# An adaLN transformer block on one core: the condition vector loaded as one row, its silu placed between the layernorm statistics, and one planned step moved later

## The chip, the core and the metric

The kernel runs on 1 core of one Trainium2 chip. The metric is the time of one execution on the device in microseconds (us). Before the change it is 761.05 us, the median of 3 runs (759.68 to 762.66). About half a per cent, 3.8 us, can be told from no change with such runs.

Names used throughout: PE is the matrix engine (PEld its weight load), DVE the vector engine, ACT the scalar engine, POOL the general engine, SP the engine that here only issues transfers. Each of them works through a list of instructions of its own, in order. SPq, ACTq and POOLq in a view are the issues of transfers by SP, ACT and POOL.

## What is computed

A block of 2048 tokens of width 512: layernorm, modulated by a condition vector c; attention with 32 heads of 16; a gated residual; again a modulated layernorm; a feed-forward layer of 1376 with gelu; a gated residual.

```python
mod = (_silu(c) @ w_mod).reshape(c.shape[0], 6, 1, -1)
sa, ca, ga, sb, cb, gb = (mod[:, i].copy() for i in range(6))
h = _layernorm(x, axis=-1) * (1 + ca) + sa
x = x + ga * _A_ref(h, A_wqkv, A_wo)      # softmax attention, then wo
h = _layernorm(x, axis=-1) * (1 + cb) + sb
x = x + gb * _B_ref(h, B_w1, B_b1, B_w2, B_b2)   # gelu MLP
return x
```

c has 512 numbers. Only sa and ca (the first 1024 columns of w_mod) are needed before the first attention scores; the rest of mod is needed later.

## The kernel before

**Tiling.** Tokens are in four blocks b of 512 (four tiles of 128), the width in four chunks of 128 (NC = 4). Activations are kept transposed (hT, kT: width on the partitions, tokens along the row). A *quad* is four heads of equal parity in one chunk for one token block; there are 32 quads of 16 key tiles, the last four of them in halves.

**Prologue (lines 128 to 384), written in order by hand.** SP and ACT each issue two tiles of x block 0 (line 140) and half of W_m0, the first 1024 columns of w_mod (line 143). Between the two, POOL issues the load of c into cc_bf, four numbers on each of 128 partitions (line 141): element j*128 + p of c goes to partition p, column j. PE meanwhile runs WARM[0] = 16 products of zeros (turn_over, line 348); WARM[1] is not used. DVE makes small masks from pidx, which POOL writes after its issue of c, and then takes the statistics of the four x tiles (line 353). Behind the second of these, SP's next loads are released: W_k, W_q, x block 1, W_v, x blocks 2 and 3, and a further part of w_mod (lines 355 to 362). ln_rstd aggregates them on DVE (line 203) and takes the root on POOL (lines 208 and 209). Then silu_c (lines 181 to 186): exp(-c) on ACT, and add, reciprocal and product on DVE give sc_bf. first_mod_mm (line 231) multiplies the columns of W_m0 with sc_bf in 32 one-column products on PE, into psm, a part of PSUM bank 7. Then for each x tile DVE normalises (line 217) and PE transposes (line 371); first_mod (lines 246 and 247) and hT_evac (lines 257 and 260) apply the modulation; PE makes the first k and q (line 379). So on PE's list stand, in order: the warming products, the 32 products with W_m0, sixteen transposes, eight products with W_k and W_q.

**The planned part (from line 386).** All that follows is ordered by a planner which runs when the program is built. It keeps a clock for each engine (`clk`), gives every step a duration in ns, and at each moment emits a step for the engine whose clock stands earliest. A dictionary `rdy` says from which time on a result may be used; a step is emitted only when all that it needs is ready by these times. So a number in `rdy` sets where in an engine's list the step that uses the result will stand, and on the chip the step waits there for the true event. Score tiles are computed by PE (line 902) and turned into weights by ACT with exp (line 1379, two or three tiles at once) or by DVE with integer arithmetic (lines 1523 and 1557). Which of the two gets a tile is decided as the plan goes, from DVE's planned load. PE then multiplies with the values (line 1141) into bank 7. Zero products (line 1222) are put in where PE would be idle.

**End of a quad (emit_out, line 1462).** DVE copies the result to o_sb (line 1472). The row of sums goes to DRAM (line 1477, d1) and back as a 128-partition piece `dall` (line 1479), both issued by SP. `rdy[("dall", qi)]` (line 1487) says when DVE may take the reciprocal (line 1491, in `back`); its result goes to DRAM and is spread over the partitions in `rb` (lines 1493 and 1496). When that is due (6500 ns later by the plan), POOL multiplies (line 1500) and adds (line 1503) into OT, which the output projection of the block uses later.

**open_late (line 556)** is a planned POOL step, run once when the weights of the prologue are no longer needed. It issues the loads of W_1 and W_2 (1376 and 1280 KB) on ACT's list and four small loads on SP's (lines 567 to 575).

Of the kernel before, what the change touches and what calls it, by code (L numbers as in the profile page):

```python
# [12 lines left out]
BF16 = mybir.dt.bfloat16  # L13
FP32 = mybir.dt.float32
# [6 lines left out]
P = 128  # L21
S = 2048
D = 512
F = 1376
H = 32
NC = 4
# [38 lines left out]
ROOT = 1000.0  # L65
ROOT_L = 700.0
SPREAD = (0.9, 0.9, 0.65)
WARM = (16, 3)
FRONT = (1200.0, 0.0, 2600.0, 4000.0)
AHEAD = 32  # L70
T_KEEP = 3
# [22 lines left out]
def adaln_block(ctx: ExitStack, tc: tile.TileContext, A_x, A_wqkv, A_wo, B_x, B_w1, B_b1, B_w2, B_b2,  # L94
                c, w_mod, out):
    nc = tc.nc
# [3 lines left out]
    const = ctx.enter_context(tc.tile_pool(name="const", bufs=1))  # L100
# [4 lines left out]
    kT = res.tile([P, NC, S], BF16, name="kT")  # L105
# [17 lines left out]
    def load_mod(i, eng):  # L123
        t = prom.tile([P, NC, 2 * D], BF16, name="W_m")
        eng.dma_start(out=t, in_=wm_v[:, :, 2 * i * D:2 * (i + 1) * D])
        return t

    xb = [prox.tile([P, 4, D], BF16, name="xb") for _ in range(NQB)]
    cc_bf = const.tile([P, NC], BF16, name="cc_bf")
# [5 lines left out]
    still = kT[:, NC - 1, S - 512:S]  # L135
    nc.vector.memset(still, 0.0)
    W_m0 = prom.tile([P, NC, 2 * D], BF16, name="W_m")
    for i, eng in enumerate((nc.sync, nc.scalar)):
        for t in (2 * i, 2 * i + 1):
            eng.dma_start(out=xb[0][:, t, :], in_=x_tok[0][:, t, :])  # L140
    nc.gpsimd.dma_start(out=cc_bf, in_=c.rearrange("o (j p) -> p (o j)", p=P))
    for i, eng in enumerate((nc.sync, nc.scalar)):
        eng.dma_start(out=W_m0[:, 2 * i:2 * i + 2, :], in_=wm_v[:, 2 * i:2 * i + 2, 0:2 * D])

# [33 lines left out]
    scf = const.tile([P, NC], FP32, name="scf")  # L178
    scb = prow.tile([P, NC, P], BF16, name="scb")

    def silu_c():
        ce = const.tile([P, NC], FP32, name="ce")
        nc.scalar.activation(out=ce, in_=cc_bf, func=ACT.Exp, scale=-1.0)
        nc.vector.tensor_scalar(out=ce, in0=ce, scalar1=1.0, scalar2=None, op0=ALU.add)
        nc.vector.reciprocal(out=ce, in_=ce)
        nc.vector.tensor_tensor(out=sc_bf, in0=cc_bf, in1=ce, op=ALU.mult)
# [25 lines left out]
    def ln_rstd(st, n):  # L212
        mv = ln_mean(st, n)
        return mv, ln_root(mv, n)
# [26 lines left out]
    def first_mod_mm(ps):  # L241
        mod_cols(ps, W_m0, 0, 0)
        mod_cols(ps, W_m0, D, 4)
# [85 lines left out]
    def bk(i, dt=FP32, n=512):  # L329
        if dt is BF16:  # L330
            return PS[:, i, 0:n // 2].bitcast(BF16)
        return PS[:, i, 0:n]
# [12 lines left out]
    dall = const.tile([P, NQB * 8, 16], FP32, name="dall")  # L345
    def turn_over(n):
        for _ in range(n):
            nc.tensor.matmul(out=PS[0:32, 6, :], lhsT=zero, rhs=still, start=True, stop=True)

    turn_over(WARM[0])  # L350
    st0 = pron.tile([P, 12, 6], FP32, name="st1")
    for t in range(4):
        seen = nc.vector.bn_stats(out=st0[:, t, :], in_=xb[0][:, t, :])
        if t == 1:
            held = nc.sync.dma_start(out=W_k, in_=wqkv_v[:, :, D:2 * D])
            tc.add_manual_dep(held.ins, seen.ins.name, AFTER, reason="order of loads")
            nc.sync.dma_start(out=W_q, in_=wqkv_v[:, :, 0:D])
            nc.sync.dma_start(out=xb[1], in_=x_tok[1])
            nc.sync.dma_start(out=W_v, in_=wqkv_v[:, :, 2 * D:3 * D])
            for b in range(2, NQB):  # L360
                nc.sync.dma_start(out=xb[b], in_=x_tok[b])
            W_m1 = load_mod(1, nc.sync)
    psm = bk(7, FP32, 16)
    mv0, rs0 = ln_rstd(st0, 4)
    silu_c()
    first_mod_mm(psm)
    turned = [bk(2 + j, BF16) for j in range(NC)]
    for t in range(4):
# [43 lines left out]
    rdy = {}  # L412
# [14 lines left out]
    def op(eng, dur, fn, label, needs=(), pos=0):  # L427
        s = Step("op", eng, dur, fn, needs, label, pos)
        alone.append(s)
        return s  # L430
# [122 lines left out]
    for j in range(NC):  # L553
        op("POOL", 1220.0, gate(lambda: W_o, j, ga_b), ("wo", j), ["ga"] + ([("wo", j - 1)] if j else []))

    def open_late():
        pro.close()
        lw = ctx.enter_context(tc.tile_pool(name="latew", bufs=1, side="right"))
        W_1 = lw.tile([P, NC, FPAD], BF16, name="W_1")
        nc.gpsimd.memset(W_1[:, :, F:FPAD], 0.0)  # L560
        nc.scalar.dma_start(out=W_1[:, :, 0:F], in_=B_w1.rearrange("(j p) n -> p j n", p=P))
        W_2 = lw.tile([P, NFC, D], BF16, name="W_2")
        lr = F - (NFC - 1) * P
        nc.gpsimd.memset(W_2[:, NFC - 1, :], 0.0)
        nc.scalar.dma_start(out=W_2[:, 0:NFC - 1, :],
                            in_=B_w2[0:(NFC - 1) * P, :].rearrange("(j p) n -> p j n", p=P))
        nc.sync.dma_start(out=W_2[0:lr, NFC - 1, :], in_=B_w2[(NFC - 1) * P:F, :])
        b1_bf = lw.tile([P, NFC], BF16, name="b1_bf")
        nc.gpsimd.memset(b1_bf, BIG)
        nc.sync.dma_start(out=b1_bf[:, 0:NFC - 1], in_=B_b1[0:(NFC - 1) * P].rearrange("(j p) -> p j", p=P))  # L570
        nc.sync.dma_start(out=b1_bf[0:lr, NFC - 1:NFC],
                          in_=B_b1[(NFC - 1) * P:F].rearrange("(p o) -> p o", o=1))
        b1c = lw.tile([P, NFC], FP32, name="b1c")
        nc.gpsimd.tensor_copy(out=b1c, in_=b1_bf)
        nc.sync.dma_start(out=W_2[lr:lr + 1, NFC - 1, :], in_=B_b2.rearrange("(o f) -> o f", o=1))
        nc.gpsimd.tensor_scalar(out=W_2[lr:lr + 1, NFC - 1, :], in0=W_2[lr:lr + 1, NFC - 1, :], scalar1=1.0 / BIG,
                                scalar2=None, op0=ALU.mult)
        clk["ACT"] += 120.0
        late.update(W_1=W_1, W_2=W_2, b1c=b1c)
        tl = ctx.enter_context(tc.tile_pool(name="tailp", bufs=1, side="right"))  # L580
        tl2 = ctx.enter_context(tc.tile_pool(name="tailp2", bufs=2, side="right"))
        late.update(tl=tl, tl2=tl2)
# [270 lines left out]
    clk = {"PE": 0.0, "ACT": 650.0, "DVE": 950.0, "POOL": 0.0}  # L853
# [608 lines left out]
    def emit_out(qi, t):  # L1462
        hf = None if qi < LAST else (qi - LAST) // HV
        if hf is not None and (qi - LAST) % HV >= HV - 2:
            return emit_half(qi, t)
        b, tq = quads[qi]
        ch, par = divmod(tq, 2)
        cs = tok_of(qi)
        n = cs.stop - cs.start
        f = n // 32  # L1470
        o = osp.tile([P, 512], FP32, name="o_sb")
        made = nc.vector.tensor_copy(out=o[:, cs], in_=PS[:, 7, cs])  # L1472
        clk["DVE"] = t + 67.0 + 1.042 * n
        dve_log.append((clk["DVE"], made))
        od_free[0] = clk["DVE"] + L_DVE
        d1 = scr.tile([4, n], FP32, name="d1" if hf is None else "dh")
        nc.sync.dma_start(out=d1, in_=o.rearrange("(r e) n -> r e n", e=32)[:, 16 - par, cs])
        den = dall[:, tq + 8 * b, f * (hf or 0):f * (hf or 0) + f]
        nc.sync.dma_start(out=den, in_=d1.rearrange("r (p f) -> (r p) f", f=f))
        rb = RB[par]  # L1480
        if par == 0 and not hf:
            if (b, ch) == (1, 0) and FIRST < NC:
                OT[(b, ch)] = odp.tile([P, 512], BF16, name="OT1")
            else:
                OT[(b, ch)] = otp.tile([P, 512], BF16, name="OT")
        ot = OT[(b, ch)]
        rdy[("dall", qi)] = clk["DVE"] + 6000.0

        def back():
            rp = osp.tile([P, 16], FP32, name="rp")  # L1490
            nc.vector.reciprocal(out=rp[:, 0:f], in_=den)
            d2 = scr.tile([4, n], FP32, name="d2" if hf is None else "di")
            nc.sync.dma_start(out=d2.rearrange("r (p f) -> (r p) f", f=f), in_=rp[:, 0:f])
            for r in range(4):
                rows = slice(32 * r + 16 * par, 32 * r + 16 * par + 16)
                nc.sync.dma_start(out=rb[rows, cs], in_=d2[r:r + 1, :].to_broadcast([16, n]))
            rdy[("rb", qi)] = clk["DVE"] + 6500.0

        def mult():
            return nc.gpsimd.tensor_tensor(out=(o if par else ot)[:, cs], in0=o[:, cs], in1=rb[:, cs], op=ALU.mult)  # L1500

        def both():
            return nc.gpsimd.tensor_tensor(out=ot[:, cs], in0=ot[:, cs], in1=o[:, cs], op=ALU.add)  # L1503

        long = 60.0 + 2.27 * n
        alone.insert(0, Step("op", "DVE", 170.0, back, [("dall", qi)], ("rp", qi)))
        alone.insert(0, Step("op", "POOL", long, mult, [("rb", qi)], ("oo" if par else "oe", b, ch, hf)))
        if par:
            alone.insert(0, Step("op", "POOL", long, both, [("oe", b, ch, hf), ("oo", b, ch, hf)],
                                 ("ot", b, ch) if hf is None else ("ot", b, ch, hf)))  # L1510
# [180 lines left out]
    while cur[0] < QN or outs or sums or evacs or alone:  # L1691
        e = min(clk, key=lambda x: (clk[x], rank[x]))
        t = clk[e]
# [51 lines left out]
```

## Time and profile before

| | us |
|---|---|
| median of 3 runs | 761.05 |
| the profiled execution | 759.09 |
| its span, first to last instruction | 757.2 |
| PE busy | 737.4 |
| ACT busy | 720.6 |
| DVE busy | 701.0 |
| POOL busy | 110.6 |

The profile is of one execution. Times in it are from the span's start. A row of the timeline is: start, duration, engine, line of the kernel, operation, output<-input, shape, count; in brackets the time for which the engine was idle before it, and what ended that. A row of the windows is: stretch, its length, busy time of PE, PEld, DVE, ACT and POOL with counts, the granted PE clock (1.00 is full), the busy share of the 16 DMA engines, and GB/s. The chain of waits is followed back from the last instruction, at each step to whatever released it.

### The profile page before, as it was taken

What the parts mean: (1) busy time and instruction counts of PE and PEld (TensorE: products, weight loads), DVE (VectorE), ACT (ScalarE), POOL (GpSimd) and SP (SyncE); (2) the same over time, 40 slices, a digit from 0 to 9 for tenths busy, and PEclk for the clock granted to TensorE, in tenths of its full rate; (3) what the DMA queues carried; (4) which work ended last, traced back from release to release, by engine and by line L of the source; (5) the groups of instructions that cost most, each with busy time, mean ns of one, the idle gap of its engine ahead of it and who ended that gap; (6) DMA issues with size and microseconds to landing.
All of it is one profiled execution on the core that took longest, in us unless ns stands there. A gap on an engine that the chain in (4) does not pass through costs nothing.

```text
span 757.2 us, 21449 instructions
## 1 busy us (share of the span) xinstructions
PE 737.4 (97%) x8885; PEld 259.4 (34%) x8888; DVE 701.0 (93%) x1455; ACT 720.6 (95%) x732; POOL 110.6 (15%) x137
## 2 busy tenths in 40 slices
PE   6999999999899999999999999999999999999997
PEld 3432333233233333223332232332233322444444
DVE  4966999999799999999999999999999999999984
ACT  1999999999899999999999999999999999999993
POOL 3334100211032311101001110100101110010010
PEclk8999999999999999999999999999999999999999
DMA  8300000000500100000001000000001000000000
GB/s 281 109 2 3 16 5 11 7 10 21 148 10 9 38 9 3 10 9 10 17 13 48 10 10 9 10 6 24 22 11 51 10 24 10 17 22 14 5 9 31
DMA packets 27960, 20.49 MB, mean 27 GB/s; under 512 B 14049, under 2 KB 23906, under 8 KB 27858
## 3 DMA queue, kind: packets, MB, share of 16 engines
q1 hardware_dynamic: 25442, 15.57, 7.2%
q10 hardware_dynamic: 2384, 3.51, 1.5%
q8 instruction: 71, 1.16, 0.6%
q14 instruction: 31, 0.25, 0.1%
q0 software_dynamic: 32, 0.00, 0.0%
HBM read 16.45 MB, written 2.61 MB: 25 GB/s over the span
## 4 chain that ended last, share of the span: by engine, by line
PE 64%; ACT 22%; DVE 5%; issue 5%; DMA 2%; SPq 0%; DVEq 0%; ACTq 0%
PE PS L902 22%; PE PS L1141 21%; ACT PB L1379 21%; PE PS L435 14%; PE PS L1222 3%; DVE TB L1523 3%; DVE TB L1557 2%; PE PS L770 2%; PE PS L799 1%; DMA W_m<-in_w_mod_dram 1%; DMA d<-o_sb 1%; ACT uG L649 1%; PE PS L1225 1%; PE PS L222 1%; ACT L1379 0%
## 5 line engine op out<-in xcount | busy, mean ns | idle before, releaser
L1379 ACT ACTIVATE PB<-PS 128x1024 bf16<-128x1024 f32 (+1 forms) x687 | 673.3, 1211 | 8.3 <-PE PS L902 4.6
L1523 DVE TENSOR_SCALAR TB<-PS 128x512 int16<-128x512 f32 (+1 forms) x538 | 369.5, 700 | 11.7 <-PE PS L902 9.5
L902 PE MATMUL PS<-qm,kT 32*128 32x512 bf16 (+1 forms) x2304 | 293.2, 359 | 5.4 <-ACT PB L1379 4.0
L1141 PE MATMUL PS<-PB,VE 128*32 128x512 bf16 (+1 forms) x1654 | 254.0, 361 | 0.0
L1141 PE MATMUL PS<-TB,VV 128*32 128x512 f16 (+1 forms) x1252 | 221.3, 360 | 1.8 <-DVE TB L1557 1.8
L1557 DVE TENSOR_SCALAR TB<-TB 128x1024 int16<-128x1024 int16 x556 | 219.9, 419 | 3.3
L902 PEld LDWEIGHTS <-kT 32*128 32x128 bf16 x2304 | 83.1, 91 | 253.6 <-issue 249.0
L1141 PE MATMUL PS<-TB,VE 128*32 128x512 f16 (+2 forms) x650 | 148.6, 361 | 0.2 <-DVE TB L1523 0.2
L1141 PEld LDWEIGHTS <-VE 128*32 128x32 bf16 x2304 | 72.4, 94 | 81.3 <-issue 75.3
L1222 PE MATMUL PS<-W_q,zero 128*32 128x256 bf16 x497 | 96.2, 274 | 1.3 <-DVE TB L1523 0.9
L1141 PEld LDWEIGHTS <-VV 128*32 128x32 bf16 x1252 | 57.3, 95 | 39.9 <-issue 36.6
L1222 PEld LDWEIGHTS <-zero 128*32 128x32 bf16 x497 | 46.0, 96 | 33.7 <-issue 11.1
L1500 POOL TENSOR_TENSOR OT<-o_sb,rb 128x512 bf16<-128x512 f32 (+1 forms) x16 | 19.3, 1203 | 248.4 <-DVE TB L1557 134.8
L1500 POOL TENSOR_TENSOR o_sb<-o_sb,rb 128x512 f32<-128x512 f32 (+1 forms) x16 | 19.3, 1204 | 223.4 <-DVE TB L1557 204.4
L435 PE MATMUL PS<-h2T,W 128*32 128x512 bf16 x528 | 47.3, 383 | 0.0
L435 PE MATMUL PS<-W,uG 128*32 128x512 bf16 x528 | 46.4, 383 | 0.0
L639 DVE TENSOR_SCALAR uG<-PS,b1c 128x512 bf16<-128x512 f32 x33 | 24.5, 742 | 0.0
L1503 POOL TENSOR_TENSOR OT<-OT,o_sb 128x512 bf16<-128x512 bf16 (+1 forms) x16 | 17.6, 1100 | 32.3 <-DVE TB L1557 30.1
L435 PE MATMUL PS<-W_o,OT 128*32 128x512 bf16 x272 | 22.2, 383 | 0.0
L1472 DVE COPY o_sb<-PS 128x512 f32<-128x512 f32 (+1 forms) x32 | 20.7, 647 | 0.9 <-PE PS L1141 0.8
L308 POOL TENSOR_SCALAR VV<-VE 128x512 bf16<-128x512 bf16 x12 | 18.0, 1502 | 20.7 <-DVE VE L303 12.5
L435 PE MATMUL PS<-hT,W_k 128*32 128x512 bf16 x240 | 20.9, 385 | 0.0
(124 smaller groups left out, 418.0 us busy)
## 6 DMA issues: line engine op xcount, KB each, us to landing
rb<-d SPq DMA_DIRECT2D x112, 32.0 KB
W_m<-in_w_mod_dram SPq DMA_DIRECT2D x2, 1024.0 KB
out_dram<-ob SPq DMA_DIRECT2D x16, 128.0 KB
xb<-in_A_x_dram SPq DMA_DIRECT2D x3, 512.0 KB
xr<-in_A_x_dram SPq DMA_DIRECT2D x3, 512.0 KB
W<-in_B_w_dram ACTq DMA_DIRECT2D x1, 1376.0 KB
W<-in_B_w_dram ACTq DMA_DIRECT2D x1, 1280.0 KB
W_m<-in_w_mod_dram ACTq DMA_DIRECT2D x1, 512.0 KB
```

What stands on the lines that cost most here:

```text
L308: return nc.gpsimd.tensor_scalar(out=dst, in0=src, scalar1=WJ[j], scalar2=None, op0=ALU.mult)
L435: nc.tensor.matmul(out=ps[cols, :], lhsT=lhsT[:, cols], rhs=rhs, start=start, stop=stop)
L639: return lambda ps, e: nc.vector.tensor_scalar(out=T["u"][:, fc, :], in0=ps, scalar1=late["b1c"][:, fc:fc + 1], scalar2=None, op0=ALU.add)
L902: nc.tensor.matmul(out=bk(bank)[:, seg(qi, i)], lhsT=kT[32 * r:32 * r + 32, ch, kt[i] * P:(kt[i] + 1) * P], rhs=qm[(b, ch)][32 * r:32 * r ...
L1141: nc.tensor.matmul(out=PS[32 * r:32 * r + 32, 7, tok_of(qi)], lhsT=wt, rhs=src[:, seg(qi, i)], start=not started[qi][r], stop=todo[qi][r] ...
L1222: nc.tensor.matmul(out=PS[0:32, b_, 0:256], lhsT=zero, rhs=W_q[:, 0, 0:256], start=True, stop=True)
L1379: nc.scalar.activation(out=dst, in_=PS[:, b0:b0 + n, :], func=ACT.Exp, bias=-KEXP * math.log(2.0), scale=math.log(2.0) / STEP)
L1472: made = nc.vector.tensor_copy(out=o[:, cs], in_=PS[:, 7, cs])
L1500: return nc.gpsimd.tensor_tensor(out=(o if par else ot)[:, cs], in0=o[:, cs], in1=rb[:, cs], op=ALU.mult)
L1503: return nc.gpsimd.tensor_tensor(out=ot[:, cs], in0=ot[:, cs], in1=o[:, cs], op=ALU.add)
L1523: made = nc.vector.tensor_scalar(out=TB[:, u["a"]["s"], i:i + n, :], in0=PS[:, b0:b0 + n, :], scalar1=T_BIAS, scalar2=0.0, op0=ALU.add, op ...
L1557: made = nc.vector.tensor_scalar(out=TB[:, s, 0:n, :], in0=TB[:, a["s"], 0:n, :], scalar1=float(MJ[j] - MJ[j - 1]), scalar2=None, op0=ALU.add)
```

## The change

Five edits, in three places.

- *The load of c.* It becomes one row of 512 numbers on one partition (cc_row, a piece of kT that is written later), issued first on ACT's list instead of on POOL's. A one-element tile `one` is set by DVE.
- *Row to columns.* Four products of a 1x128 piece of the row with `one` put c on 128 partitions, four columns, into columns 8 to 11 of psm (silu_in); DVE copies them to cc_bf (silu_exp).
- *Order of silu.* The copy and the exp come after the first of the four statistics, the rest (silu_out) after the third.
- *Warming products.* 6 before silu_in and 9 behind it, instead of 16.
- *A due time in the plan.* open_late notes POOL's planned time. A quad copied out between 4 us before and 14 us after it has its sums due 11 us after the copy instead of 6 us.

```diff
-WARM = (16, 3)
+WARM = (6, 9)
...
+    cc_row = kT[0:1, NC - 2, S - D:S]
+    one = const.tile([1, 1], BF16, name="one")
+    nc.vector.memset(one, 1.0)
+    nc.scalar.dma_start(out=cc_row, in_=c)
     for i, eng in enumerate((nc.sync, nc.scalar)):
         for t in (2 * i, 2 * i + 1):
             eng.dma_start(out=xb[0][:, t, :], in_=x_tok[0][:, t, :])
-    nc.gpsimd.dma_start(out=cc_bf, in_=c.rearrange("o (j p) -> p (o j)", p=P))
...
-    def silu_c():
-        ce = const.tile([P, NC], FP32, name="ce")
+    ce = const.tile([P, NC], FP32, name="ce")
+
+    def silu_in(psm):
+        for j in range(NC):
+            nc.tensor.matmul(out=psm[:, 8 + j:9 + j], lhsT=cc_row[:, j * P:(j + 1) * P], rhs=one, start=True, stop=True)
+
+    def silu_exp(psm):
+        nc.vector.tensor_copy(out=cc_bf, in_=psm[:, 8:8 + NC])
         nc.scalar.activation(out=ce, in_=cc_bf, func=ACT.Exp, scale=-1.0)
+
+    def silu_out():
         nc.vector.tensor_scalar(out=ce, in0=ce, scalar1=1.0, scalar2=None, op0=ALU.add)
...
     turn_over(WARM[0])
+    psm = bk(7, FP32, 16)
+    silu_in(psm)
+    turn_over(WARM[1])
     st0 = pron.tile([P, 12, 6], FP32, name="st1")
     for t in range(4):
         seen = nc.vector.bn_stats(out=st0[:, t, :], in_=xb[0][:, t, :])
-        if t == 1:
+        if t == 0:
+            silu_exp(psm)
+        elif t == 2:
+            silu_out()
+        elif t == 1:
             held = nc.sync.dma_start(out=W_k, in_=wqkv_v[:, :, D:2 * D])
...
-    psm = bk(7, FP32, 16)
     mv0, rs0 = ln_rstd(st0, 4)
-    silu_c()
     first_mod_mm(psm)
...
+    late_at = [0.0]
+
     def open_late():
...
         late.update(W_1=W_1, W_2=W_2, b1c=b1c)
+        late_at[0] = clk["POOL"]
...
-        rdy[("dall", qi)] = clk["DVE"] + 6000.0
+        rdy[("dall", qi)] = clk["DVE"] + (11000.0 if late_at[0] - 4000.0 <= t < late_at[0] + 14000.0 and late_at[0] else 6000.0)
```

## The prediction, made before the changed kernel was run

> **What bounds the kernel now.** I read the page first: the span, how full the engines are, the chain that ended last by line.
>
> ```profile
> span 757.2 us, 21449 instructions
> PE 737.4 (97%) x8885; PEld 259.4 (34%) x8888; DVE 701.0 (93%) x1455; ACT 720.6 (95%) x732; POOL 110.6 (15%) x137
> PE PS L902 22%; PE PS L1141 21%; ACT PB L1379 21%; PE PS L435 14%; PE PS L1222 3%; DVE TB L1523 3%; DVE TB L1557 2%; PE PS L770 2%; PE PS L799 1%; DMA W_m<-in_w_mod_dram 1%; DMA d<-o_sb 1%; ACT uG L649 1%; PE PS L1225 1%; PE PS L222 1%; ACT L1379 0%
> ```
>
> Three engines are over 90% busy at once, so no one of them sets the time: over most of the span the list that the planner wrote does. But two transfers stand on the chain, W_m and d<-o_sb. The chain in order of time places them (start, length):
>
> ```profile
> 1.68 9.01 DMA W_m<-in_w_mod_dram
> ...
> 190.58 6.48 DMA d<-o_sb
> 197.08 1.66 DMA dall<-d
> ```
>
> The diff edits the code around both places, so each is read in the timeline. First the stretch in which W_1 and W_2 are loaded (start, length; in brackets the idle time ahead and what ended it), and under it two one-microsecond windows (the last two numbers are the DMA share and GB/s):
>
> ```profile
> 187.96 0.68 DVE L1472 COPY o_sb<-PS 128x512 f32<-128x512 f32 x1
> 190.10 0.39 SPq L575 DMA_DIRECT2D W<-in_B_b_dram  x1
> 190.58 0.52 SPq L1477 DMA_DIRECT2D d<-o_sb  x1
> 195.94 0.42 DVE L1557 TENSOR_SCALAR TB<-TB 128x1024 int16<-128x1024 int16 x1
> 198.83 0.25 DVE L1491 RECIPROCAL rp<-dall 128x16 f32<-128x16 f32 x1 [2.48 <-DMA dall<-d]
> 199.42 0.38 PE L1141 MATMUL PS<-TB,VV 128*32 128x512 f16 x1 [1.61 <-DVE TB L1557]
> 200.78 2.37 ACT L1379 ACTIVATE PB<-PS 128x1536 bf16<-128x1536 f32 x2 [1.75 <-PE PS L902]
> 210.09 1.27 POOL L1500 TENSOR_TENSOR OT<-o_sb,rb 128x512 bf16<-128x512 f32 x1 [10.26 <-DVE TB L1557]
> 210.47 0.68 DVE L1472 COPY o_sb<-PS 128x512 f32<-128x512 f32 x1
> ```
>
> ```profile
> 193.00:194.00 1.00, 1.00 (x24) 0.29 (x16) 0.72 (x1) 1.00 (x2) 0.00 (x0) 1.00 1.20 304
> 198.00:199.00 1.00, 0.00 (x0) 0.00 (x0) 0.17 (x1) 1.00 (x2) 0.91 (x2) 1.00 0.09 8
> ```
>
> The reader should see one small round trip held up by two large loads. The quad's sums are copied out at 187.96; their row goes to DRAM at 190.58, behind the four small loads of line 567 to 575 on SP's list; with the DMA engines full (share 1.20) it takes 6.48 us, and the way back 1.66. DVE's list reaches the reciprocal when the step before it ends (195.94 + 0.42 = 196.36) and stands there for 2.48 us. All that is queued behind it stands too: PE, short of a shifted tile from DVE, for 1.61 us, then ACT, short of scores from PE, for 1.75 us. That is a stall of the whole machine, not idle time of one engine.
>
> Then the prologue:
>
> ```profile
> 0.73 0.88 ACTq L140 DMA_DIRECT2D xb<-in_A_x_dram  x2
> 1.21 5.12 PE L348 MATMUL PS<-kT,zero 128*32 128x512 bf16 x16 [1.21 <-DVE kT L136]
> 1.24 0.99 POOL L141 DMA_DIRECT2D cc_bf<-in_c_dram  x1 [0.81 <-POOLq L1728]
> 3.61 2.52 DVE L353 BATCH_NORM_STATS2 st<-xb 128x6 f32<-128x512 bf16 x4
> 4.97 0.37 SPq L355 DMA_DIRECT2D W_k<-in_A_wqkv_dram  x1
> 7.30 1.04 POOL L209 TENSOR_TENSOR rs<-rs,half 128x4 f32<-128x4 f32 x1
> 8.64 0.20 ACT L183 ACTIVATE ce<-cc_bf 128x4 f32<-128x4 bf16 x1 [5.23 <-DMA cc_bf<-in_c_dram]
> 9.30 0.16 DVE L186 TENSOR_TENSOR sc_bf<-cc_bf,ce 128x4 bf16<-128x4 bf16 x1
> 9.38 1.38 DVE L217 TENSOR_SCALAR xb<-xb,mv,rs 128x512 bf16<-128x512 bf16 x4
> 10.74 0.99 PE L231 MATMUL PS<-sc_bf,W_m 128*128 128x1 bf16 x32 [4.41 <-DMA W_m<-in_w_mod_dram]
> 11.59 1.87 PE L371 MATMUL PS<-ident,xb 128*128 128x128 bf16 x16
> 15.01 0.63 PE L379 MATMUL PS<-hT,W_q 128*128 128x512 bf16 x1
> 15.43 0.63 PE L379 MATMUL PS<-hT,W_k 128*128 128x512 bf16 x1
> ```
>
> c lands late: ACT waits 5.23 us for it and silu is done at 9.46. But W_m lands at 10.69, and PE, which has the products of line 231 ahead of the transposes, waits for W_m, not for silu. So an earlier c alone buys nothing: of the 7.4 us from POOL's issue to ACT's exp all is under W_m's 9.01.
>
> **Part 1: the reciprocal's planned time.** The plan reads dall 6.0 us after the copy; the new line makes that 11.0 when the copy falls between 4 us before and 14 us after open_late on the planner's clock. SP's list has line 1477 right behind line 575, so this quad is emitted after open_late and within about a microsecond of it; the next copy comes 22.5 us later (210.47) and falls outside. So one step of 0.25 us moves, by 5.0 us of plan. DVE would reach it near 196.36 + 5.0 = 201.4, and dall is there at 197.08 + 1.66 = 198.74: 2.6 us to spare. The wait of 2.48 us goes. What that is worth: PE's stall was 1.61, ACT's 1.75, DVE's 2.48. I take 2.0, between ACT's and DVE's, since all three run on without a gap. Ends: 2.5 (DVE's whole wait) and 0 (another wait takes its place). Moved with the reciprocal, and after it on SP's list, are one DMA of line 1493 and four of line 1496. Late next are the broadcast rb and POOL's product at 210.09, which in the plan needs rb 6.5 us after the reciprocal: 201.4 + 6.5 = 207.9, still ahead of 210.09; and the product that uses the output is far off:
>
> ```profile
> L435 PEld LDWEIGHTS <-OT x272: 91/96/98, 271.9 to 736.9; 128*32 128x32 bf16 x136
> ```
>
> Were that cover gone, POOL would be up to 5 us later and PE with it.
>
> **Part 2: the prologue.** Removed: POOL's issue of 0.99 us. So pidx, which DVE's masks wait for, comes about 1 us sooner, but the first statistics also wait for x. Added on ACT's list ahead of its two x tiles: one issue of 0.44 us (0.88 for two). x tiles 2 and 3 and ACT's half of W_m go out 0.44 later. Added on PE: four products of one column, by line 231's 32 in 0.99 us some 0.12 us, behind six warming products instead of sixteen; nine more follow, so one fewer in all. If the row lands like the first x tiles (issued from 0.73, read by DVE at 3.61), PE hardly stands for it: six products at 0.32 (line 348's mean) to 0.43 (line 379's spacing, 15.01 to 15.43) end between 3.1 and 3.8. Behind that wait on PE stand only warming products and line 231. Added on DVE between the statistics: a copy of 0.16, and three silu steps moved forward with their gaps, 0.6. The copy waits for PE and stands ahead of the second statistic, which releases W_k: from 4.97 to about 5.2; behind W_k on SP's list wait W_q, xb and W_v. The later statistics end some 0.8 later, POOL's root by 8.34 + 0.8 = 9.1, and the norms, which stood behind silu until 9.38, can start then. All of it lies under W_m, due at 10.69; without that cover it would be 0.8 us on the path.
>
> So the term is W_m's landing. Two rows of the DMA queues, in 6 to 8.5 us and in 8.5 to 11 us:
>
> ```profile
> q0 software_dynamic: 25, 0.00, 9.1%
> ```
>
> ```profile
> q10 hardware_dynamic: 20, 0.03, 3.3%
> ```
>
> c's packets (q0) took 9.1% of 16 engines in 2.5 us, 3.6 engine-us or 0.23 us each, just before the last 20 packets of ACT's W_m half (q10). Without them these could land 0.23 sooner, or more if they all fell to the late engines; 0.44 later if ACT's issue decides. If W_m came so early that the norms bind (end near 9.1 + 1.4 = 10.5, the last four transposes a quarter of 1.87), the transposes end at 11.0 instead of 13.46: at most 2.5 gained. Ends: -2.5 and +0.5; nearest row is q0's, and I take -0.3.
>
> By the Trainium skill (DMA: Bandwidth & Descriptors, Issuing engines are not separate DMA queues), the transfers of SP, ACT and POOL run on the same 16 engines and another issuer saves only issue time; this speaks against a gain here, and the sum by it would be 0.3 us less. The trace only shows that q0's packets took engine time.
>
> **Part 3: the rest of the list.** One step moved at 196 makes the planner draw everything after it anew. The trace does not price that. The nearest row, DVE's waits for scores (us in total, times, longest):
>
> ```profile
> DVE TB L1523 <- PE PS L902: 9.5, 22, 1.1
> ```
>
> These are gaps of 0.43 us; five more or fewer of them are 2.1 us. I take 0, ends -2 and +3.
>
> **Sum.** -2.0 - 0.3 + 0 = -2.3 us. The profiled execution took 759.09 us (1.9 more than its span), so it would take 756.8. It was 1.96 below the median of 761.05; the same difference from the median gives 758.7.
>
> **Rivals.** *A, the stall goes and the prologue gains too* (756.1). If W_m lands sooner and the second warming block ends late, PE's gap of 4.41 us shrinks and the half clock that follows it may not come:
>
> ```profile
> 11.00:12.00 1.00, 1.00 (x33) 1.00 (x31) 0.23 (x2) 0.00 (x0) 0.00 (x0) 0.57 1.10 347
> ```
>
> At full clock line 379's eight products save 8 x 0.21 = 1.7 and the sixteen transposes half of 1.87, together 2.6: 758.7 - 2.6. For it: nine products at 0.43 from 4.2 end at 8.1, a gap of some 2.6. Against it: sixteen ended at 6.33 before, and fifteen with four small ones between them should end near there, so that the gap stays; and the trace does not show how short a gap is short enough.
>
> The Trainium skill (TensorE: Matmul & The Clock Gate, Part 1: The HAM clock gate) puts that at about 3.4 us: an idle window so long brings half clock. The trace agrees so far, 4.41 us idle and then 0.57.
>
> *B, hidden anyway* (760.7). The stall's time comes back as other waits, or the plan emits the quad outside the new window, and only the 0.3 is left. For it: the list has waits enough into which a delay can fall (part 3's row). Against: all three stop together, and SP's order shows open_late ahead.
>
> *C, slower* (763.4). The redrawn list gives ACT more score tiles. Each tile is taken by ACT or DVE by DVE's planned load. A tile costs ACT the difference of these two forms (count | busy, mean ns):
>
> ```profile
> L1379 ACT ACTIVATE PB<-PS 128x1024 bf16<-128x1024 f32 x590 | 564.6, 1152 | 2.1 <-PE PS L902 1.2 <-PE PS L1141 0.6
> L1379 ACT ACTIVATE PB<-PS 128x1536 bf16<-128x1536 f32 x96 | 151.4, 1577 | 6.2 <-PE PS L902 3.3 <-PE PS L1141 1.6 <-issue 1.3
> ```
>
> That is 0.425 us on an engine 95% busy. From 6 tiles on (2.5 us) the gain is used up; 11 more are 4.7, so 758.7 + 4.7 = 763.4. For it: ACT has no slack. Against: DVE's amount of work changes by nothing.
>
> **How the numbers follow.** Forecast 0.50, A 0.22, B 0.15, C 0.13. Half a per cent of 761.05 is 3.8 us, about what a measurement of this kernel can tell: faster is under 757.2, slower over 764.9. Faster: four fifths of A and a quarter of the forecast (a lucky list), 0.18 + 0.12 = 0.30. Slower: half of C and a little of the forecast's tail, 0.08. Same: 0.62. The forecast's own range, with 0.8 around the stall and 2 for the list, is 756 to 761; reaching to A and most of C it is 754.8 to 763.0.
>
> **What would show it.** Right: no wait ahead of line 1491 near 200, no PE or ACT gap of 1.6 to 1.8 there, neither d<-o_sb nor dall<-d on the chain; exp of c before 5.5 with PE still waiting for W_m near 10.5; DVE and ACT counts at line 1523 and 1379 within a few. Wrong: the same gap in another line (B), line 379's products 0.21 apart (A), ACT's tiles up by six or more (C), or the copy ahead of the second statistic standing over 1 us for PE, which would move W_k.

## The result, and the profile after

The changed kernel takes 754.24 us (median of 7 runs, 753.61 to 757.45) against 761.05 before; the ratio is 0.9919, with a 95% interval of 0.9900 to 0.9938. That is 6.2 us less (4.7 to 7.6). The prediction said 758.7, so 2.3 less, with a range from 754.8: the sign was right, the gain was nearly three times as large, and the median lies 0.6 us below the range. Taken from the ratio, which compares with times of the kernel before from the same session, it is 754.9, just inside. The profiled execution took 753.81 us. The head of its page:

```profile
span 752.0 us, 21400 instructions
PE 737.2 (98%) x8864; PEld 258.1 (34%) x8867; DVE 703.4 (94%) x1447; ACT 721.6 (96%) x742; POOL 109.5 (15%) x136
```

Work did not shrink: PE is busy as long as before (737.4), DVE and ACT 2.4 and 1.0 us longer (701.0, 720.6). What went is idle time. The timeline of the changed kernel's prologue (line numbers are its own: 242 was 231, 387 was 371, 395 was 379):

```profile
0.74 0.53 ACTq L141 DMA_DIRECT2D kT<-in_c_dram  x1
0.74 0.88 SPq L144 DMA_DIRECT2D xb<-in_A_x_dram  x2
1.29 0.84 ACTq L144 DMA_DIRECT2D xb<-in_A_x_dram  x2
...
3.87 0.26 PE L188 MATMUL PS<-one,kT 1*128 1x1 bf16 x4
4.06 3.45 PE L359 MATMUL PS<-kT,zero 128*32 128x512 bf16 x9
4.17 0.16 DVE L191 CAST cc_bf<-PS 128x4 bf16<-128x4 f32 x1 [0.60 <-PE PS L188]
...
4.96 0.37 SPq L373 DMA_DIRECT2D W_k<-in_A_wqkv_dram  x1
...
5.84 0.16 DVE L197 TENSOR_TENSOR sc_bf<-cc_bf,ce 128x4 bf16<-128x4 bf16 x1
...
7.44 1.18 PE L242 MATMUL PS<-sc_bf,W_m 128*128 128x1 bf16 x32
7.71 0.81 PEld L242 LDWEIGHTS <-W_m 128*128 128x128 bf16 x30 [0.16 <-DMA W_m<-in_w_mod_dram]
...
8.84 1.37 PE L387 MATMUL PS<-ident,xb 128*128 128x128 bf16 x16 [0.22 <-DVE xb L228]
...
11.58 0.38 PE L395 MATMUL PS<-hT,W_k 128*128 128x512 bf16 x1
...
11.80 0.38 PE L395 MATMUL PS<-hT,W_q 128*128 128x512 bf16 x1
```

W_m, not silu, is still what comes last (sc_bf is ready at 6.0), but it is there at 7.7 instead of 10.69. The second warming block runs until 7.51, so PE hardly idles, the granted clock stays at 1.00, and the k and q products follow each other in 0.21 us instead of 0.43. DVE's copy waits 0.60 us for PE and W_k's load still goes out at 4.96, because the first statistic, which waits for x, starts at 2.87 instead of 3.61. The first quad is copied out at 61.49 instead of 66.42.

Then the stretch with the loads of W_1 and W_2:

```profile
183.03 0.68 DVE L1491 COPY o_sb<-PS 128x512 f32<-128x512 f32 x1
...
186.80 0.52 SPq L1496 DMA_DIRECT2D d<-o_sb  x1
193.55 0.36 SPq L1498 DMA_DIRECT2D dall<-d  x1
196.94 0.25 DVE L1510 RECIPROCAL rp<-dall 128x16 f32<-128x16 f32 x1 [0.76 <-DMA dall<-d]
...
203.32 0.69 DVE L1491 COPY o_sb<-PS 128x512 f32<-128x512 f32 x1
```

```profile
184.31 31.56 ACT L1398 ACTIVATE PB<-PS 128x1536 bf16<-128x1536 f32 x29 [0.75 <-PE PS L921]
```

The wait is 0.76 us instead of 2.48, and ACT runs on for 31.56 us. The wait is not zero: the sums came 3.0 us later after the copy than in the profile before, and the 2.6 us to spare were used up. The issue of their row came 3.77 us behind the copy instead of 2.62, and dall needed 3.39 us from its issue to the reciprocal instead of 1.75 (197.08 to 198.83).

Up to the quad copied at 183.03 the two kernels run the same list, and there the changed one is 4.9 us ahead (187.96 - 183.03). At the end it is 5.2 ahead (757.2 - 752.0). Read so, the prologue gave nearly everything and the later due time almost nothing (theory 1 below); theory 2 is that the stall was worth its 2.0 us and the prologue gave the rest. The experiments test this, since each profile is one execution.

### The profile page after: what moved, and what is told of

It reads as the page before. It is cut to its first block, busy times and chain, and to the rows that moved or that the text cites. A ratio compares the mean times of both kernels' runs of the same rounds, so it can differ in the third digit from the quotient of the medians.

```text
span 752.0 us, 21400 instructions
## 1 busy us (share of the span) xinstructions
PE 737.2 (98%) x8864; PEld 258.1 (34%) x8867; DVE 703.4 (94%) x1447; ACT 721.6 (96%) x742; POOL 109.5 (15%) x136
## 3 DMA queue, kind: packets, MB, share of 16 engines
q8 instruction: 71, 1.16, 0.7%
## 5 line engine op out<-in xcount | busy, mean ns | idle before, releaser
L921 PE MATMUL PS<-qm,kT 32*128 32x512 bf16 (+1 forms) x2304 | 296.6, 358 | 5.2 <-ACT PB L1398 2.4
L1160 PE MATMUL PS<-PB,VE 128*32 128x512 bf16 (+1 forms) x1649 | 249.7, 361 | 0.0
L1576 DVE TENSOR_SCALAR TB<-TB 128x1024 int16<-128x1024 int16 (+1 forms) x560 | 223.6, 421 | 4.5
L1160 PE MATMUL PS<-TB,VV 128*32 128x512 f16 (+1 forms) x1262 | 217.2, 359 | 0.0
L1160 PE MATMUL PS<-TB,VE 128*32 128x512 f16 (+2 forms) x655 | 150.9, 360 | 0.0
L1160 PEld LDWEIGHTS <-VE 128*32 128x32 bf16 x2304 | 70.1, 94 | 77.3 <-issue 70.8
L1241 PE MATMUL PS<-W_q,zero 128*32 128x256 bf16 x467 | 91.7, 273 | 2.0 <-DVE TB L1542 1.1
L1241 PEld LDWEIGHTS <-zero 128*32 128x32 bf16 x467 | 42.4, 96 | 32.8 <-issue 11.3
```

The costliest lines, as they stand in the source:

```text
L921: nc.tensor.matmul(out=bk(bank)[:, seg(qi, i)], lhsT=kT[32 * r:32 * r + 32, ch, kt[i] * P:(kt[i] + 1) * P], rhs=qm[(b, ch)][32 * r:32 * r ...
L1160: nc.tensor.matmul(out=PS[32 * r:32 * r + 32, 7, tok_of(qi)], lhsT=wt, rhs=src[:, seg(qi, i)], start=not started[qi][r], stop=todo[qi][r] ...
L1241: nc.tensor.matmul(out=PS[0:32, b_, 0:256], lhsT=zero, rhs=W_q[:, 0, 0:256], start=True, stop=True)
L1576: made = nc.vector.tensor_scalar(out=TB[:, s, 0:n, :], in0=TB[:, a["s"], 0:n, :], scalar1=float(MJ[j] - MJ[j - 1]), scalar2=None, op0=ALU.add)
```

## The experiments

**The two parts apart, the old load put back, and the kernel before once more.** The kernel before with only the later due time:

```diff
+    late_at = [0.0]
     def open_late():
...
-        rdy[("dall", qi)] = clk["DVE"] + 6000.0
+        rdy[("dall", qi)] = clk["DVE"] + (11000.0 if late_at[0] - 4000.0 <= t < late_at[0] + 14000.0 and late_at[0] else 6000.0)
```

> The kernel before with only the later due time of the sums. Theory 1 (the prologue gave nearly the whole gain): the wait ahead of the reciprocal shrinks from 2.5 us to 0 to 1 us, as in the changed kernel, but the list drawn anew gives most of it back, so about 760.7 us, no more than 1 us under the kernel before. Theory 2 (the prediction's term of 2.0 us holds and the rest is prologue): about 759 us.

Measured: 757.58, ratio 0.9970 (0.9953 to 0.9987), so 2.3 us less than the kernel before (1.0 to 3.6). Theory 2 holds for this part. DVE's row in this kernel has no wait:

```profile
199.28 0.24 DVE L1494 RECIPROCAL rp<-dall 128x16 f32<-128x16 f32 x1
```

The changed kernel with the old due time:

```diff
-        rdy[("dall", qi)] = clk["DVE"] + (11000.0 if late_at[0] - 4000.0 <= t < late_at[0] + 14000.0 and late_at[0] else 6000.0)
+        rdy[("dall", qi)] = clk["DVE"] + 6000.0
```

> The changed kernel with the sums due after 6 us again, so only the prologue is changed. Theory 1: the list after the prologue is that of the kernel before and everything runs 4.9 us sooner, the wait of about 2.5 us ahead of the reciprocal is back, and the time is about 756 us (761.05 - 4.9). Theory 2: about 758 us, with the first quad copied out some 3 us sooner than before instead of 4.9.

Measured: 758.4, ratio 0.9976 (0.9959 to 0.9994), 1.8 us less. The seventh quad is copied at 184.93, 3.0 sooner than in the profile before, as theory 2 said; but the wait that stayed is larger than the expectation had it:

```profile
197.48 0.25 DVE L1510 RECIPROCAL rp<-dall 128x16 f32<-128x16 f32 x1 [5.01 <-DMA dall<-d]
```

The kernel before, unchanged:

> The kernel before, profiled a second time. If the late W_m is a property of the kernel, PE starts on it at 10 to 11 us again; if it was the chance of one execution, at another time, down to 9.5 us, where silu ends.

One time, 761.86. Again PE starts on W_m's products at 10.74, but here silu ends the wait, since c came later still:

```profile
9.87 0.20 ACT L183 ACTIVATE ce<-cc_bf 128x4 f32<-128x4 bf16 x1 [6.46 <-DMA cc_bf<-in_c_dram]
...
10.74 0.99 PE L231 MATMUL PS<-sc_bf,W_m 128*128 128x1 bf16 x32 [3.42 <-DVE sc_bf L186]
...
198.96 0.25 DVE L1491 RECIPROCAL rp<-dall 128x16 f32<-128x16 f32 x1 [3.70 <-DMA dall<-d]
```

So the wait for the sums was 2.48, 3.70 and 5.01 us in three profiles with the old due time: the profile on which the prediction rests had the mildest. Theory 1 falls: the list drawn anew does not eat the gain.

The mildest differs in more than the wait. In the other five profiles with the old due time the granted clock fell to half behind the stall, after gaps of PE of 1.80 to 4.14 us, and by the windows stayed there for some 3.5 to 10 us; in the profile before, with a gap of 1.61, and in all eight with a later due time it stayed at 1.00. The same window in the kernel before, in the one without a load of c (wait 2.75, below) and in the changed one:

```profile
202.00:203.00 1.00, 0.92 (x7) 0.36 (x6) 0.96 (x3) 1.00 (x2) 0.00 (x0) 1.00 0.31 62
```

```profile
202.00:203.00 1.00, 1.00 (x5) 0.21 (x5) 0.48 (x2) 0.14 (x1) 0.00 (x0) 0.50 0.03 4
```

```profile
202.00:203.00 1.00, 1.00 (x7) 0.30 (x6) 1.00 (x4) 1.00 (x2) 0.06 (x1) 1.00 0.00 0
```

The times agree with this. In 73 later executions of the kernel before, the mean clock over the span, which takes in the prologue, was 0.987 to 0.998; the median time is 761.7 us in the 14 at 0.989 or less and 758.7 in the 11 at 0.994, and the two at 0.998 took 755.6 and 757.4. The changed kernel had 0.996 to 0.999 in all seven. A good part of the gain thus goes with the clock falling less often; how much of it the clock by itself makes is not shown.

The changed kernel plus the old load of c, into a tile that nobody reads:

```diff
+    cc_x = const.tile([P, NC], BF16, name="cc_x")
+    nc.gpsimd.dma_start(out=cc_x, in_=c.rearrange("o (j p) -> p (o j)", p=P))
```

> The changed kernel plus the old load of c (four numbers per partition, issued by POOL) into a tile that nobody reads. Theory 1 (that load held up the DMA engines that were late with W_m): W_m is needed and waited for until 9.5 us or later again, and the time rises by 2 to 4 us to 756 to 758. Rival (the load of c never touched W_m, which came sooner for another reason, such as the order of issues or chance): PE starts on W_m at about 7.5 us and the time stays at 754.2.

Measured: 756.18, ratio 0.9944 (0.9926 to 0.9963). The time is in theory 1's range, W_m is not: its second half ends its wait at 8.57, not 9.5 or later. So the old load explains less than a third of W_m's 3 us. Whether it has a price in time is not settled: the interval overlaps that of the changed kernel, and in this profile the clock was at half from 10 to 13 us, which in the changed one it was not.

**What brings W_m sooner.** Three kernels separate the load of c from the order of ACT's issues. The changed kernel with the row issued by POOL:

```diff
-    nc.scalar.dma_start(out=cc_row, in_=c)
+    nc.gpsimd.dma_start(out=cc_row, in_=c)
```

> The changed kernel with the row of c issued by POOL instead of ACT; still one row. If the shape of the old load (four single numbers for each of 128 partitions) held up the other loads, the DMA engines move about 3.3 MB in the first 12 us, as in the changed kernel (3.4) and unlike the one before (2.9), and the time stays within 1.5 us of 754.2. If POOL's queue as such held them up, it is as with the old load put back: 3.1 MB or less and 756 us or more. If what helped was ACT's two tiles and half of W_m going out 0.5 us later, 2.9 MB.

The kernel before with its four numbers per partition issued by ACT:

```diff
-    nc.gpsimd.dma_start(out=cc_bf, in_=c.rearrange("o (j p) -> p (o j)", p=P))
+    nc.scalar.dma_start(out=cc_bf, in_=c.rearrange("o (j p) -> p (o j)", p=P))
```

> The kernel before with its load of c, four numbers per partition, issued by ACT behind its two x tiles instead of by POOL. If the shape held up the other loads, about 2.9 MB in the first 12 us again, W_m waited for until 10 us or later, and 760 to 761 us. If POOL's queue did, 3.2 MB or more, PE starts on W_m by 9.5 us, and the time is 758 to 759.

The kernel before with no load of c at all:

```diff
-    nc.gpsimd.dma_start(out=cc_bf, in_=c.rearrange("o (j p) -> p (o j)", p=P))
+    nc.vector.memset(cc_bf, 0.05)
```

> The kernel before with the load of c left out: cc_bf is set to a constant by DVE, so c itself is not used. Nothing goes through POOL's queue, and ACT's tiles go out together with SP's as before. If POOL's load was what held W_m up, about 3.3 MB move in the first 12 us and PE starts on W_m by 8.5 us; the time is 757 to 758. If the cause is that SP's and ACT's first loads go out at the same moment, 2.9 MB, W_m at 10 us or later, and 760 or more.

Measured: 758.09 (ratio 0.9961, 0.9944 to 0.9979), 760.09 (0.9995, 0.9981 to 1.0009) and 760.1 (0.9991, 0.9975 to 1.0007). The last is the strongest: with the load of c gone no gain can be told, and W_m is about as late as before:

```profile
0.74 0.88 ACTq L140 DMA_DIRECT2D xb<-in_A_x_dram  x2
0.74 0.90 SPq L140 DMA_DIRECT2D xb<-in_A_x_dram  x2
...
10.22 0.95 PE L231 MATMUL PS<-sc_bf,W_m 128*128 128x1 bf16 x32 [3.36 <-DMA W_m<-in_w_mod_dram]
```

And with the row on POOL, so that ACT's tiles go out with SP's again (the row also lands later, and W_k's load goes out at 5.76 instead of 4.96):

```profile
9.71 1.01 PE L242 MATMUL PS<-sc_bf,W_m 128*128 128x1 bf16 x32 [0.83 <-DMA W_m<-in_w_mod_dram]
```

MB moved by all queues in the first 12 us, and the end of the last wait for W_m:

| | ACT's first tile with SP's (0.74) | ACT's first tile 0.55 us later |
|---|---|---|
| a load of c on POOL | 2.86 MB, 10.7 us (before); 2.73, 10.7 (before again); 2.90, 10.0 (due time only); 3.10, 9.7 (row on POOL) | 3.13 MB, 8.6 us (old load put back) |
| none on POOL | 2.91 MB, 10.2 us (no load); 2.86, 10.1 (columns on ACT) | 3.39 MB, 7.7 us (after); 3.32, 8.1 (prologue only); 3.41, 8.0 (due after 14 us); 3.36, 7.9 (six warming products) |

The step from left to right is 1.1 to 2.5 us of W_m. From top to bottom it is 0.5 to 0.9 in the right column, and nothing clear in the left. By its 3.10 MB and its time the row on POOL met what was expected if POOL's queue were the cause, not the 2.9 MB expected for ACT's delay. But the two kernels of the lower left cell have nothing on that queue, and their W_m was late all the same. A window of 7 to 8 us (DMA share and GB/s last) shows the same in three kernels: without a load of c, with the old load put back, and changed:

```profile
7.00:8.00 1.00, 0.00 (x0) 0.00 (x0) 0.11 (x1) 0.00 (x0) 0.85 (x1) 1.00 0.67 236
```

```profile
7.00:8.00 1.00, 0.51 (x4) 0.11 (x2) 0.87 (x5) 0.00 (x0) 0.08 (x2) 1.00 1.04 385
```

```profile
7.00:8.00 1.00, 0.92 (x16) 0.41 (x15) 0.00 (x0) 0.00 (x0) 0.92 (x2) 1.00 1.07 360
```

In the first of them the DMA engines are not short of bytes to move, since W_m is outstanding until 10.2; they have gaps. (With the columns on ACT the gap lies earlier, at 4 to 5 us.) What goes with the gain is a side effect of the edit: the row on ACT's list puts ACT's tiles 0.55 us and its half of W_m 0.5 us behind SP's. The first x tile shows it too: where DVE's first statistic waited for it, it started at 2.87 to 2.97 us in the six kernels with ACT behind and at 3.55 to 3.69 in the three with both together. The delay of W_m's half alone does not do it: with the columns on ACT that half went out at 2.13, as late as in the changed kernel (2.16), and W_m was waited for until 10.1, though there ACT's queue also carried the 512 single numbers. Delaying ACT's issues alone, in the kernel before, was not tried. So the cause is argued, not shown, and why two queues that start together leave the engines idle later is open.

**The warming products.** The changed kernel without the second block, with all fifteen products ahead of the row's, and the kernel before with 36:

```diff
-WARM = (6, 9)
+WARM = (6, 0)
```

> The changed kernel without the nine warming products behind the row's products. If the second block is what keeps the clock up (the prediction's rival A), PE idles from 4.2 to 7.5 us, the first k and q products run 0.43 us apart instead of 0.21, and the time rises by about 2 us to 756. If the clock there is chance, 754.2 as before the edit.

```diff
-WARM = (6, 9)
+WARM = (15, 0)
```

> The changed kernel with all fifteen warming products ahead of the row's four products. If the split matters through DVE (the copy of c stands ahead of the second statistic and waits for PE), the copy waits until PE is through with fifteen products, at 6 to 7.5 us instead of 4.2; W_k's load goes out 2 to 3 us later, the norms start 2 to 3 us later, and the time rises by 1.5 to 3 us. If W_m and the clock alone decide, no change.

```diff
-WARM = (16, 3)
+WARM = (36, 3)
```

> The kernel before with 36 warming products instead of 16, so that PE is busy until W_m comes. If the clock is decided by PE's idle time, it stays full from 5 us on, the first k and q products run 0.21 us apart and the first quad is copied out about 2 us sooner than in the kernel before (66.4 and 65.9 us in its two profiles), that is near 64; the time is about 758.5. If not, no change.

In the profile with six products the clock is as rival A had it, granted 0.50 in this window against 1.00 in the changed kernel, and the k and q products are 0.43 apart (the same window of the kernel with six and of the changed one):

```profile
12.00:13.00 1.00, 1.00 (x3) 0.29 (x3) 0.00 (x0) 0.00 (x1) 0.00 (x0) 0.50 1.09 347
```

```profile
12.00:13.00 1.00, 1.00 (x8) 0.51 (x7) 0.35 (x1) 0.57 (x1) 0.00 (x0) 1.00 1.10 351
```

But the changed prologue with nine products behind the row's, in the kernel with the old due time, shows the same:

```profile
12.00:13.00 1.00, 1.00 (x3) 0.44 (x3) 0.00 (x0) 0.09 (x1) 0.00 (x0) 0.50 1.09 349
```

In the profiles the first quad comes 2.0 us later for the half clock (63.5 and 63.4 against 61.5), the seventh too, but in the kernel with six the eighth only 0.4 later: this execution had no wait ahead of the reciprocal and no gap of ACT at the loads. The time is 754.35, ratio 0.9924 (0.9901 to 0.9946), against 0.9919, not the 2 us more that were expected. The mean clock fits this: of the four executions with six products the profiled one had 0.995, the other three 0.999. So that the second block keeps the clock up is not shown; it fell in one execution with it and stayed in three without. With 36 products the kernel before has full clock and its products 0.21 apart, but the warming products run until 12.0, past W_m, a wait of 4.9 us stands ahead of the reciprocal, and the clock falls behind it: 760.57, ratio 1.0000 (0.9984 to 1.0015), inconclusive as to the time. With fifteen products ahead of the row's, the copy waits and what is released behind it waits too:

```profile
7.07 0.16 DVE L191 CAST cc_bf<-PS 128x4 bf16<-128x4 f32 x1 [3.50 <-PE PS L188]
...
7.86 0.37 SPq L373 DMA_DIRECT2D W_k<-in_A_wqkv_dram  x1
```

```profile
7.00:8.00 1.00, 0.04 (x2) 0.06 (x1) 0.93 (x3) 0.20 (x1) 0.00 (x0) 1.00 0.05 18
```

The DMA engines stand idle for want of W_k, the norms come at 11.3 instead of 8.4, and the time is 757.55, ratio 0.9963 (0.9950 to 0.9976): some 3.3 us of the gain are lost. What the split of the warming products is seen to do is to keep DVE's copy and SP's loads from waiting.

**The place of silu, and a still later due time.** The changed kernel with silu behind the statistics:

```diff
-        if t == 0:
-            silu_exp(psm)
-        elif t == 2:
-            silu_out()
-        elif t == 1:
+        if t == 1:
...
     mv0, rs0 = ln_rstd(st0, 4)
+    silu_exp(psm)
+    silu_out()
```

> The changed kernel with the copy of c's columns, the exp and the rest of silu behind the statistics and their aggregates on DVE. If W_m is what PE waits for, sc_bf comes at about 7.5 us instead of 6, PE starts on W_m's products within 0.3 us of 7.5 to 8, the norms start where they did (8.4 us, behind POOL's root) or a little sooner, and the time is unchanged, 754 to 755. If the place of silu mattered, PE starts 1 us later and the time rises by 1 us or more.

Measured: 754.62, ratio 0.9929 (0.9902 to 0.9955); PE starts on W_m at 8.00 behind sc_bf. No difference that can be told. The changed kernel with 14 us:

```diff
-clk["DVE"] + (11000.0 if
+clk["DVE"] + (14000.0 if
```

> The changed kernel with the sums due 14 us after the copy instead of 11. The wait of 0.8 us ahead of the reciprocal goes, so about 1 us less at the next copy; the list is drawn anew once more, which by the first two runs is worth some 2 us either way. Theory: 753 us, 751 to 755. Rival (the wait left at 11 us is already covered by other work): 754.2 and no change up to the next copy.

Measured: 754.83, ratio 0.9925 (0.9903 to 0.9947). The wait is gone and the next copy comes 0.64 sooner (202.68 against 203.32), but no difference in time can be told: 11 us is late enough as far as these runs show.

## Why the prediction was right in sign and short by almost two thirds

**Right.** The wait ahead of the reciprocal was a stall of the whole machine, and the later due time removes most of it. Rival B falls by the kernel with the due time alone, 2.3 us faster. Rival C falls too: ACT's instructions rose from 687 to 695 and DVE's at the line that was 1523 fell from 538 to 526, but counted in tiles ACT has two fewer (1493 and 1491) and DVE two more (555 and 557). That silu would be covered held too (silu last: no change), as did the warning that a copy standing for PE moves W_k (fifteen products). Of the signs named, PE still waiting for W_m near 10.5 did not come, products 0.21 apart (A) did, and the chain of the changed kernel cannot be read here, since its view begins only near 690 us.

**The stall, a term of 2.0: 2.3 by the times (1.0 to 3.6), 3.0 by the profiles.** From the seventh copy to the end of the span the six profiles with 6 us took 569.2 to 573.2 us, the seven with 11 us 567.6 to 569.5; the means differ by 3.0 (571.8 and 568.8), and the mean waits by 3.2 (3.6 and 0.4). The term was priced from one execution in which the wait was 2.48, the least of six (to 5.0). Its end of 2.5 for the whole wait was a bound on that execution, not on the kernel. That the term came out near is in part luck: this very execution took the 569.2, only 0.4 above the mean of the later due time. The rest goes with the clock's fall behind the stall rather than with the length of the wait (2.67 us of wait, 571.9; 5.01 us, 571.8), and the prediction did not reckon with the clock there. Whether the list drawn anew costs something that hides a larger price is not settled, so its term of 0 fits but is not shown.

**The step that failed: W_m's landing, a term of -0.3.** The prediction took c's own packets (0.23 us of each engine) as the nearest row and set the issue delay of ACT's half, 0.44, against it as a possible loss. W_m was there 3 us sooner in the profile (7.7 instead of 10.69) and 1.9 to 3.0 sooner over the kernels of the table's lower right cell than in the kernel before and the one with the due time alone (10.0 to 10.7, 7.7 to 8.1). The seventh copy is 3.1 us sooner on average: 183.0, 184.9, 183.05 and 183.3 in the four profiles with the row first on ACT, nothing on POOL's queue and both warming blocks, against 186.7 over the six of kernels built on the one before (185.9 to 188.0). Both guesses had the wrong cause. Leaving c out gains nothing; the delay of ACT's issues, which was counted as the loss, is what goes with the gain. Even the end of -2.5 was too near. It let the norms start at 9.1, behind a root of POOL that came 0.8 later; in the profile the root came no later (7.29, before 7.30), the norms started at 8.37, and the first k product at 10.67 instead of 13.77.

**Rival A** was the one that came closest (756.1): W_m came sooner and the clock stayed up, though only in three of those four profiles, and the second warming block is not shown to be the reason. Its clock term of 2.6 measured 2.0 at the first copy. Summed over both parts, 3.1 and 3.0 give 6.1, against 6.2 measured for the whole. By times the parts are 1.8 and 2.3 with intervals of about 1.3 each way, 4.1 together; whether the two help each other is not settled.

## What to carry to other kernels

A stall behind a transfer should be priced from several executions: here it was 2.5 in one and 5.0 in another of the same planned list, and the five executions in which the clock fell behind it took 2.6 to 4.0 us more from there to the end than the first. The mean clock of every execution, not only of the profiled one, shows whether an edit acts through it. When two queues load a prologue, look at the engines' gaps and not only at the order of the transfers; here an issue 0.55 us later went with a weight 1 to 2.5 us sooner. And test a suspected load by leaving it out before its removal is credited with the gain.

## What the runs showed of the hardware that was not expected

- With SP's and ACT's first loads issued together the DMA engines moved 2.7 to 3.1 MB in 12 us, with ACT 0.55 us behind 3.1 to 3.4 (2.4 where W_k's load was late, with fifteen products), and W_m came 1.1 to 2.5 us sooner in the kernels of the table. The Trainium skill (DMA: Bandwidth & Descriptors, Issuing engines are not separate DMA queues) says that a further issuer only saves issue time. By that the start of one issuer against the other would matter little; the measurement, which decides, shows a difference that goes with it, though not that the start alone makes it.
- In the kernel with six warming products PE, idle from 4.13 us, had two gaps of 2.05 and 1.54 us with 0.20 us of work between, and the clock fell to half between 7.5 and 7.75 us:

```profile
6.18 0.20 PE L242 MATMUL PS<-sc_bf,W_m 128*128 128x1 bf16 x2 [2.05 <-DMA W_m<-in_w_mod_dram]
7.92 0.96 PE L242 MATMUL PS<-sc_bf,W_m 128*128 128x1 bf16 x30 [1.54 <-DMA W_m<-in_w_mod_dram]
```

  The Trainium skill (TensorE: Matmul & The Clock Gate, Part 1) speaks of an idle window of some 3.4 us; neither gap was that long. Nor were the gaps of 0.55 and 1.16 us ahead of the half clock in the kernel with the old due time, or the ones of 1.80 and 2.28 us at the stall with the columns on ACT and without a load of c. Gaps well short of 3.4 us were thus followed by half clock here.
